# Projections split into two 64-row halves that run beside each other, with the score maxima one PSUM bank at a time

## The chip, the cores and the metric

The kernel runs on one core of one Trainium2 chip. The metric is device time in microseconds (us) of one execution of the whole program. Four compute engines matter here: TensorE (PE in the profile, its weight loads are PEld), VectorE (DVE), ScalarE (ACT) and GpSimd (POOL). SyncE (SP) issues nearly all the DMAs, in program order. Each engine works through its own instructions in program order.

## The reference

Two layers, each of them an attention block and an MLP on a 2048 x 640 tensor, all in float32:

```
qkv = layernorm(x) @ wqkv                  # 640 -> 3 x 32 heads x 20
p   = softmax(q @ k.T * 20**-0.5)          # 32 heads, 2048 x 2048 each
x   = x + (p @ v) @ wo
h   = relu(layernorm(x) @ w1 + b1) ** 2    # 640 -> 1536
x   = x + h @ w2 + b2                      # 1536 -> 640
```

The weights of both layers are the same arrays. Every float32 operand of a projection is split into a high and a low part of a shorter format, and a product is the sum of three: high by high, high by low, low by high. So a projection over 640 = 5 x 128 rows is a chain of 15 matmuls into one PSUM bank.

## The kernel before, in words

A layer has three stages: `qkv` (projections), `attention`, and `add_heads` with `mlp`. The change lies in `qkv`.

**Projections.** `UNITS` lists 40 units of q and k (128 output columns by 512 tokens); the first 16 of them (`FIRST` = 4 column blocks for four token blocks) hold what heads 0 to 11 need. `proj_unit` (L302) runs the 15 matmuls of a unit at L307, 128 rows of the array, 512 columns. Its result goes to SBUF as a high and a low part (ACT copies at L273, POOL splits at L278 and L281) and by DMA to `d_qk`. Then 16 tiles of v follow, two chains of 15 matmuls each at L358, 320 columns wide (`v_unit`, L350). The projections use PSUM banks 6 and 7 in turn.

**Maxima.** The softmax needs the largest score of each query before the attention stage uses it. It is found from scores that are computed once more, with queries on the partitions: `by_queries` (L463, matmul at L466) multiplies 60 rows, either rows 0 to 59 or rows 64 to 123 of the array (`par` = 0 or 1), by 512 keys. The two values of `par` are two heads, and two such matmuls with different `par` run side by side in the upper and the lower half of the array. A maximum over 512 keys for 128 queries of one head is called a single here; a layer has 2048 of them. Those not done in `qkv` are done in `attention` by `smax` (L474, DVE at L478).

In `qkv` there are two ways. A plain one (`smax_two`, L482): two matmuls into two neighbouring banks, one reduction of both by DVE (L487). A double one covers 1024 keys: `step_two` (L491) multiplies by the difference of two key blocks (`kd`), ACT takes the positive part (L498); `both_two` (L501) multiplies by the first block, and DVE adds the two and reduces (L508). So a double gives four singles for four matmuls, two ACT and two DVE instructions. All of these use banks 0 to 5 in three pairs (`Twos`). I call the two matmuls with `par` = 0 and 1 that belong together a pair; a double has two pairs.

**Order.** The order on TensorE is the program's. While the projections are issued, `between` (L801) counts matmuls, and after every 8.2 (`PACE`; 11 while there are no doubles) `some` (L775) issues a round: a `both`, a plain, and a `step` for the next round, three pairs in all. After every fourth matmul the next step of `rest` is issued, which prepares the normalised and transposed input (`front`, L373: statistics and normalisation on DVE, 4 transposes at L388 per step). The lists `PLAIN` and `DOUBLE` (L659, L666) say which groups of 8 pairs or doubles come up after which unit; groups that haven't come up when the projections end are left to `attention`.

**Attention.** 32 blocks of 4 heads by 512 queries. For each of 16 key tiles: four score matmuls (L563, 62 rows, two side by side), four exponentials on ACT (L570), four matmuls with v in four column tiles (L575). The order is a written-out string (`ORDERS`, L859) in which maxima are strewn, at least 12 pairs in each eight key tiles as long as any are left.

Of the kernel before, what the change touches and what calls it, by code (L numbers as in the profile page):

```python
# [8 lines left out]
F32 = mybir.dt.float32  # L9
# [7 lines left out]
P = 128  # L17
# [3 lines left out]
H = 32  # L21
# [18 lines left out]
def tile_layers(  # L40
# [51 lines left out]

    ps_st = Ring(0, 1, 2, 3)
    ps_pj = Ring(6, 7)

    class Twos:


        def __init__(self):
            self.n = 0  # L100

        def two(self):
            self.n = (self.n + 2) % 6
            return banks[:, self.n : self.n + 2, :]

        def __call__(self, label):
            return self.two()[:, 0, :]

    ps_q = Twos()
# [192 lines left out]
    def proj_unit(pos, tb, between):  # L302
        dst = ps_pj("pj")
        n = 0
        for k in range(KD):
            for hw, hx in THREE:
                nc.tensor.matmul(  # L307
                    dst,
                    w_qk.piece(pos * 10 + hw * KD + k),
                    xt_[tb][k][:, hx, :],  # L310
                    start=(n == 0),
                    stop=(n == 3 * KD - 1),
                )
                n += 1
                between()
# [34 lines left out]
    def v_unit(tt, between):  # L350
        tb, i = divmod(tt, 4)
        v = slot([P, H, 32], F32, "v")
        nc.gpsimd.memset(v[:, :, DH:], 1.0)
        n = 0
        for hf in range(2):
            dst = ps_pj("pv_")
            for j, (k, (hx, hw)) in enumerate((k, t) for k in range(KD) for t in THREE):
                nc.tensor.matmul(  # L358
                    dst[:, :HALF],
                    xt_[tb][k][:, hx, i * P : (i + 1) * P],  # L360
                    w_v.piece(k * 4 + hw * 2 + hf),
                    start=(j == 0),
                    stop=(j == 3 * KD - 1),
                )
                n += 1
                between()
            nc.scalar.copy(
                v[:, hf * 16 : hf * 16 + 16, :DH],
                dst[:, :HALF].rearrange("p (h d) -> p h d", d=DH),
            )  # L370
        return lambda: dma(nc.sync, d_v[tt * P : (tt + 1) * P], v)

    def front(tb, x_src, bank):  # L373

        rows = [row_tile(x_src, tb * 4 + i) for i in range(4)]
        yield
        mvs = []
        for x in rows:
            mvs.append(stats(x))
            yield  # L380
        for x, mv in zip(rows, mvs):
            normalise(nc.vector, x, mv)
            yield
        res = []
        for k in range(KD):
            dst = bank("xt")
            for i in range(4):
                nc.tensor.transpose(  # L388
                    dst[:, i * P : (i + 1) * P], rows[i][:, k * P : (k + 1) * P], ident
                )  # L390
            t = slot([P, 2, QB], F32R, "xnT")
            (split_on_pool if tb > 1 else split_to)(t[:, 0, :], t[:, 1, :], dst)
            res.append(t)
            if k == KD - 1:
                xt_[tb] = res
            yield

    def fronts(steps):


        for n, f in enumerate(steps):
            for m, _ in enumerate(f):
                if m == 7 and n + 1 < len(steps):
                    next(steps[n + 1])
                yield
# [76 lines left out]
    def smax_two(t, p, sub, c):  # L482

        dst = ps_q.two()
        for par in range(2):
            by_queries(dst[:, par, :], t, p, sub, c, par)
        nc.vector.tensor_reduce(  # L487
            maxima(t)[:, 2 * p : 2 * p + 2, sub, c], dst, axis=AX.X, op=ALU.max
        )

    def step_two(t, p, sub, x):  # L491

        dst = ps_q.two()
        res = [xtile("rl")[:, :QB] for _ in range(2)]
        for par in range(2):
            by_queries(dst[:, par, :], t, p, sub, x, par)
        for par in range(2):
            nc.scalar.activation(res[par], dst[:, par, :], AF.Relu)  # L498
        return res

    def both_two(t, p, sub, x, r):  # L501

        dst = ps_q.two()
        c = 2 * "de".index(x)
        for par in range(2):
            by_queries(dst[:, par, :], t, p, sub, c, par)
        for par in range(2):
            nc.vector.tensor_tensor_reduce(  # L508
                out=r[par],
                in0=dst[:, par, :],  # L510
                in1=r[par],
                scale=1.0,
                scalar=LEAST,
                op0=ALU.add,
                op1=ALU.max,
                accum_out=maxima(t)[:, 2 * p + par, sub, c : c + 1],
            )
# [125 lines left out]
    def prep_job():  # L643
# [7 lines left out]
        if jobs:  # L651
# [11 lines left out]
        ([], [(1, qb, c) for qb in (1, 2, 3) for c in (2, 3)]  # L663
         + [(2, qb, c) for qb in range(3) for c in range(NQB)]),
# [6 lines left out]
         [(1, 3, "d"), (1, 0, "e")]),  # L671
# [6 lines left out]
    PACE = 8.2  # L678
# [3 lines left out]
    def qkv(first, x_src, rest):  # L682
# [5 lines left out]
        state = {"pace": 0, "n": 0}  # L688
# [31 lines left out]
        def later(f=None):  # L720
            if f:
                pending.append(f)
            while len(pending) > (1 if f else 0):
                pending.pop(0)()

# [11 lines left out]
        def end_group(x):  # L737
            g, qb, c = x
            t = g * NQB + qb
            rest = groups + double + [w[0] for w in work + twos] + [w[0][0] for w in begun]  # L740
# [10 lines left out]
            for y in [y for y in k_t if y[0] == g < 2 and y not in use]:  # L751
                del k_t[y]
# [13 lines left out]
        def one():  # L766
            w = following(groups, work)
            if w:
                (g, qb, c), p, sub = w
                smax_two(g * NQB + qb, p, sub, c)  # L770
                done.add((g * NQB + qb, p, sub, c))
                if (p, sub) == PAIRS[-1]:
                    end_group(w[0])

        def some():  # L775
# [8 lines left out]
            if begun:  # L784
                w, r = begun.pop()
                (g, qb, x), p, sub = w
                t = g * NQB + qb
                both_two(t, p, sub, x, r)
                c = 2 * "de".index(x)
                done.update([(t, p, sub, c), (t, p, sub, c + 1)])  # L790
                if (p, sub) == PAIRS[-1]:
                    end_group(w[0])
            one()
            w = following(double, twos)
            if w:
                (g, qb, x), p, sub = w
                begun.append((w, step_two(g * NQB + qb, p, sub, x)))
            else:
                one()
# [461 lines left out]
```

## Time and profile before

| | |
|---|---|
| median of 3 runs | 3725.42 us (3721.52 to 3725.97) |
| the profiled execution | 3724.8 us, of which 3723.0 us are the span of the profile |
| granted TensorE clock | 0.997 |
| first `qkv` stage | 0 to about 361 us |
| first attention, then `add_heads` and `mlp` | to about 1449 us, to about 1878 us |
| second `qkv` stage | 1879 to 2205 us |
| second attention, then `add_heads` and `mlp` | to about 3295 us, to 3723 us |
| busy in the span | PE 3683.9, DVE 2791.9, ACT 2558.5, POOL 824.1 us |

The duration of a matmul in the profile runs from its start to its modelled end, and matmuls overlap. So the time that a matmul takes of TensorE is read from the distance of the starts, not from the duration. In the timeline, equal instructions in a row stand in one line: start, time from the first start to the last end, engine, line, operation, output and inputs, shapes, count; in brackets the idle time before and what ended it.

### The profile page before, as it was taken

Reading aid. Unit: us, or ns where it says so; the run is one execution under the profiler, and the core shown is the slowest. Engines: PE = TensorE matmul, PEld = TensorE weight load, DVE = VectorE, ACT = ScalarE, POOL = GpSimd, SP = SyncE. Lnnn points to the kernel's source line nnn. Section 1 sums busy time; section 2 is a strip of 40 time slices with the busy share of each in tenths; the row PEclk is TensorE's granted clock in tenths of the full one; section 3 lists DMA queues with packets and bytes.
Section 4 is the critical chain, followed back from the end, with each engine's and each line's share of the span. In section 5 each row is a group of like instructions: output and inputs, shape, how many; then the busy total and the mean of one; then the engine's idle time right before and its main releaser. Section 6 shows DMA issues by size and latency. Waiting matters only on the chain.

```text
span 3723.0 us, 64229 instructions
## 1 busy us (share of the span) xinstructions
PE 3683.9 (99%) x23572; PEld 2111.6 (57%) x23572; DVE 2791.9 (75%) x4799; ACT 2558.5 (69%) x4891; POOL 824.1 (22%) x914
## 2 busy tenths in 40 slices
PE   7999999999999999999999999999999999999999
PEld 5677344433443346989876763444334433378998
DVE  7788999999999993344567889999999999823443
ACT  2455999999999995122224459999999999941221
POOL 6430234322112211111153201121212121201110
PEclk9999999999999999999999999999999999999999
DMA  7564454432212136511265533222222111373111
GB/s 228 186 211 142 136 153 139 132 107 74 59 52 52 43 94 204 200 43 43 81 221 172 171 124 81 75 72 56 72 78 57 45 48 49 107 246 139 43 48 38
DMA packets 256531, 402.28 MB, mean 108 GB/s; under 512 B 67580, under 2 KB 114428, under 8 KB 256216
## 3 DMA queue, kind: packets, MB, share of 16 engines
q1 hardware_dynamic: 255384, 395.80, 34.3%
q8 instruction: 187, 3.06, 0.3%
q10 hardware_dynamic: 832, 2.37, 0.2%
q14 instruction: 128, 1.05, 0.1%
HBM read 261.22 MB, written 136.81 MB: 107 GB/s over the span
## 4 chain that ended last, share of the span: by engine, by line
PE 94%; DVE 3%; ACT 1%; DMA 1%; POOL 0%; issue 0%; SPq 0%; ACTq 0%; DVEq 0%; POOLq 0%
PE banks L575 27%; PE banks L296 20%; PE banks L563 20%; PE banks L466 15%; PE banks L307 6%; PE banks L358 4%; DVE mx L487 1%; DVE h L267 1%; PE banks L1047 0%; DVE bst L254 0%; DVE r L1074 0%; ACT h L266 0%; PE banks L388 0%; ACT r L1073 0%; DMA k<-d_qk 0%
## 5 line engine op out<-in xcount | busy, mean ns | idle before, releaser
L570 ACT ACTIVATE e<-banks 128x512 f32<-128x512 f32 x4096 | 2114.3, 604 | 63.4 <-PE banks L563 3.9
L478 DVE TENSOR_REDUCE mx<-banks 128x1 f32<-128x512 f32 x2940 | 1846.5, 684 | 188.1 <-PE banks L466 115.5
L466 PE MATMUL banks<-k,q 60*128 60x512 f32 x3744 | 1157.4, 436 | 5.4 <-DMA q<-d_qk 3.0
L563 PE MATMUL banks<-q,k 62*128 62x512 f32 x4096 | 1151.5, 435 | 2.1 <-DVE mx L487 1.7
L575 PE MATMUL banks<-e,vg 128*32 128x512 f32 x8192 | 1092.9, 605 | 0.1
L563 PEld LDWEIGHTS banks<-q,k 62*128 62x128 f32 x4096 | 600.5, 185 | 699.2 <-ACT e L570 665.8
L466 PEld LDWEIGHTS banks<-k,q 60*128 60x128 f32 x3744 | 537.4, 185 | 333.5 <-DVE mx L478 206.3
L296 PE MATMUL banks<-w,h 128*128 128x320 f32 x2304 | 360.0, 313 | 8.0 <-DVE h L267 4.3
L575 PEld LDWEIGHTS banks<-e,vg 128*32 128x32 f32 x8192 | 161.6, 108 | 358.2 <-issue 331.6
L498 ACT ACTIVATE rl<-banks 128x512 f32<-128x512 f32 x352 | 191.3, 596 | 247.9 <-PE banks L466 247.8
L296 PEld LDWEIGHTS banks<-w,h 128*128 128x128 f32 x2304 | 342.3, 189 | 17.4 <-DVE h L267 8.6
L296 PE MATMUL banks<-xnT,w 128*128 128x512 f32 x1440 | 330.0, 389 | 0.0
L307 PE MATMUL banks<-xnT,wqk 128*128 128x512 f32 x1200 | 319.8, 409 | 0.8 <-ACT xnT L266 0.4
L1073 ACT ACTIVATE r<-banks,b_t 128x512 f32<-128x512 f32 x96 | 66.1, 689 | 364.3 <-PE banks L296 362.9
L508 DVE CUSTOM_DVE_ANT_0 rl<-banks,rl 128x512 f32<-128x512 f32 x352 | 229.2, 689 | 112.4 <-PE banks L466 103.0
L296 PEld LDWEIGHTS banks<-xnT,w 128*128 128x128 f32 x1440 | 269.5, 188 | 55.2
L487 DVE TENSOR_REDUCE mx<-banks 128x2 f32<-128x1024 f32 x226 | 271.7, 1220 | 15.1 <-PE banks L466 14.3
L307 PEld LDWEIGHTS banks<-xnT,wqk 128*128 128x128 f32 x1200 | 217.0, 191 | 86.2 <-issue 43.3
L619 POOL TENSOR_TENSOR few<-few,minus_t 128x16 f32<-128x16 f32 x62 | 179.8, 2901 | 289.2 <-DMA few<-d_s 289.2
L630 POOL TENSOR_TENSOR o<-o 128x512 f32<-128x512 f32 x62 | 79.6, 1283 | 620.7 <-DMA o<-d_r 350.8
L1093 DVE TENSOR_TENSOR x<-banks,x 128x320 f32<-128x320 f32 x128 | 62.9, 492 | 184.4 <-PE banks L296 184.2
L278 POOL CAST mr<-nt 128x32 fp32r<-128x32 f32 x64 | 13.4, 210 | 801.5 <-DVE nt L534 801.5
(77 smaller groups left out, 1994.4 us busy)
## 6 DMA issues: line engine op xcount, KB each, us to landing
q<-d_qk SPq DMA_DIRECT2D x744, 80.0 KB
d_qk<-ev SPq DMA_DIRECT2D x80, 512.0 KB
k<-d_qk SPq DMA_DIRECT2D x468, 80.0 KB
x<-d_x SPq DMA_DIRECT2D x88, 320.0 KB
d_o<-ot SPq DMA_DIRECT2D x248, 80.0 KB
ot<-d_o SPq DMA_DIRECT2D x38, 512.0 KB
d_v<-v SPq DMA_DIRECT2D x32, 512.0 KB
vg<-d_v SPq DMA_DIRECT2D x32, 512.0 KB
```

What stands on the lines that cost most here:

```text
L296: nc.tensor.matmul(dst, a, b, start=(n == 0), stop=(n == last))
L307: nc.tensor.matmul(dst, w_qk.piece(pos * 10 + hw * KD + k), xt_[tb][k][:, hx, :], start=(n == 0), stop=(n == 3 * KD - 1),)
L358: nc.tensor.matmul(dst[:, :HALF], xt_[tb][k][:, hx, i * P : (i + 1) * P], w_v.piece(k * 4 + hw * 2 + hf), start=(j == 0), stop=(j == 3 * K ...
L466: nc.tensor.matmul(dst, q_t[t][b : b + 60, p, sub * P : (sub + 1) * P], k_t[t // NQB, c][b : b + 60, p, :], start=True, stop=True,)
L478: nc.vector.tensor_reduce(maxima(t)[:, 2 * p + par, sub, c : c + 1], dst, axis=AX.X, op=ALU.max)
L487: nc.vector.tensor_reduce(maxima(t)[:, 2 * p : 2 * p + 2, sub, c], dst, axis=AX.X, op=ALU.max)
L498: nc.scalar.activation(res[par], dst[:, par, :], AF.Relu)
L508: nc.vector.tensor_tensor_reduce(out=r[par], in0=dst[:, par, :], in1=r[par], scale=1.0, scalar=LEAST, op0=ALU.add, op1=ALU.max, accum_out= ...
L563: nc.tensor.matmul(dst, k_t[t // NQB, kt // 4][b : b + 62, p, (kt % 4) * P : (kt % 4 + 1) * P], q_t[t][b : b + 62, p, :], start=True, stop ...
L570: nc.scalar.activation(es[p][:, par, :], dst, AF.Exp, scale=SCALE)
L575: nc.tensor.matmul(acc[32 * h : 32 * h + 32, :], v_t[t // NQB, kt // 8][:, kt % 8, 32 * h : 32 * h + 32], es[p][:, par, :], start=(kt == 0 ...
L619: nc.gpsimd.tensor_tensor(few, few, minus_t, op=ALU.pow)
```

## The change

Every projection matmul with 128 rows becomes two with 64 rows: one for the upper half of the rows (0 to 63), one for the lower half. `chains` lists all 40 units and the 32 chains of v. Two counters run over them. The upper counter is ahead: an iteration issues the next upper half-matmul of chain n, and then the next lower half-matmul of an earlier chain, which adds to the bank that the upper rows of that chain have left. The lower counter follows 15 + 9 half-matmuls behind (`LAG` = 9). Between the last upper and the first lower half-matmul of a chain stands a tiny ACT copy (`mark`): it waits for the one, and the other waits for it. A chain of 15 matmuls becomes 30; there are 72 chains and 72 marks in a layer.

The maxima are now issued one matmul at a time (`single`): the one with `par` = 0 takes the place of an upper half-matmul, the one with `par` = 1 that of a lower one. Projections get the four banks 4 to 7, maxima (and the transposes of `front`) banks 0 to 3, one each. The counted pace is gone; `insert` keeps clocks (`now`) for PE, DVE and ACT in microseconds, written as constants (0.235 or 0.155 for an iteration, 0.58 to 0.7 for the work on a bank), and issues a matmul for a maximum only when the bank that comes next is free by these clocks. Up to two doubles are begun at a time. A plain is now two reductions of one bank each.

Of the `PLAIN` list four groups remain (64 singles a layer); all else that is listed for heads 0 to 11 is now `DOUBLE`, 22 groups instead of 11 (704 singles instead of 352). Fronts that run inside `qkv` make their transposes for two banks in one step, three steps in place of five.

The diff, cut to its core:

```
-    ps_pj = Ring(6, 7)
-
-    class Twos:
-
-
-        def __init__(self):
-            self.n = 0
-
-        def two(self):
-            self.n = (self.n + 2) % 6
-            return banks[:, self.n : self.n + 2, :]
-
-        def __call__(self, label):
-            return self.two()[:, 0, :]
-
-    ps_q = Twos()
+    ps_pj = Ring(4, 5, 6, 7)
+    ps_q = Ring(0, 1, 2, 3)
...
-    def proj_unit(pos, tb, between):
-        dst = ps_pj("pj")
-        n = 0
-        for k in range(KD):
-            for hw, hx in THREE:
-                nc.tensor.matmul(
-                    dst,
-                    w_qk.piece(pos * 10 + hw * KD + k),
-                    xt_[tb][k][:, hx, :],
-                    start=(n == 0),
-                    stop=(n == 3 * KD - 1),
-                )
-                n += 1
-                between()
...
+    def after(later, earlier):
+        tc.add_manual_dep(
+            later.ins,
+            earlier.ins.name,
+            mybir.DependencyInfo(mybir.DependencyClass.Sync, mybir.DependencyReason.DATA),
+            reason="lower rows add to the bank that the upper rows have left",
+        )
+
+    def product(ch, n, r):
+
+        what, a, b = ch["of"]
+        rows = slice(64 * r, 64 * r + 64)
+        k, t = divmod(n, 3)
+        if what == "qk":
+            hw, hx = THREE[t]
+            w = w_qk.piece(b * 10 + hw * KD + k)[rows]
+            x = xt_[a][k][rows, hx, :]
+            pair, width = (w, x), QB
+        else:
+            tb, i = divmod(a, 4)
+            hx, hw = THREE[t]
+            x = xt_[tb][k][rows, hx, i * P : (i + 1) * P]
+            pair, width = (x, w_v.piece(k * 4 + hw * 2 + b)[rows]), HALF
+        first, last = r == 0 and n == 0, r == 1 and n == 3 * KD - 1
+        if first:
+            ch["dst"] = ps_pj("pj")
+        m = nc.tensor.matmul(ch["dst"][:, :width], *pair, start=first, stop=last)
+        if n == 3 * KD - 1 and r == 0:
+            mark = nc.scalar.copy(mark_t[:, 0:1], mark_t[:, 1:2])
+            after(mark, m)
+            ch["upper"] = mark
+        if n == 0 and r == 1:
+            after(m, ch.pop("upper"))
+
+    def end_qk(pos, tb, dst):
...
+    def end_v(tt, hf, dst):
+        if hf == 0:
+            vs[tt] = slot([P, H, 32], F32, "v")
+            nc.gpsimd.memset(vs[tt][:, :, DH:], 1.0)
+        nc.scalar.copy(
+            vs[tt][:, hf * 16 : hf * 16 + 16, :DH],
+            dst[:, :HALF].rearrange("p (h d) -> p h d", d=DH),
+        )
+        if hf:
+            v = vs.pop(tt)
+            return lambda: dma(nc.sync, d_v[tt * P : (tt + 1) * P], v)
...
+    def front(tb, x_src, bank, each=1):
...
+        for k0 in range(0, KD, each):
+            ks = range(k0, min(k0 + each, KD))
+            dsts = [bank("xt") for _ in ks]
+            for k, dst in zip(ks, dsts):
+                for i in range(4):
+                    nc.tensor.transpose(
+                        dst[:, i * P : (i + 1) * P], rows[i][:, k * P : (k + 1) * P], ident
+                    )
+            for dst in dsts:
+                t = slot([P, 2, QB], F32R, "xnT")
+                (split_on_pool if tb > 1 else split_to)(t[:, 0, :], t[:, 1, :], dst)
+                res.append(t)
+            if len(res) == KD:
                 xt_[tb] = res
-            yield
+                rows.clear()
+            yield 0, len(res) < KD
...
-    def smax_two(t, p, sub, c):
-
-        dst = ps_q.two()
-        for par in range(2):
-            by_queries(dst[:, par, :], t, p, sub, c, par)
-        nc.vector.tensor_reduce(
...
+    def step_one(t, p, sub, x, par):
+
+        dst = ps_q("sm")
+        res = xtile("rl")[:, :QB]
+        by_queries(dst, t, p, sub, x, par)
+        nc.scalar.activation(res, dst, AF.Relu)
+        return res
...
+    def both_one(t, p, sub, x, par, r):
+
+        dst = ps_q("sm")
+        c = 2 * "de".index(x)
+        by_queries(dst, t, p, sub, c, par)
+        nc.vector.tensor_tensor_reduce(
+            out=r,
+            in0=dst,
+            in1=r,
+            scale=1.0,
+            scalar=LEAST,
+            op0=ALU.add,
+            op1=ALU.max,
+            accum_out=maxima(t)[:, 2 * p + par, sub, c : c + 1],
...
-        ([], [(1, qb, c) for qb in (1, 2, 3) for c in (2, 3)]
-         + [(2, qb, c) for qb in range(3) for c in range(NQB)]),
+        ([], []),
...
-         [(1, 3, "d"), (1, 0, "e")]),
+         [(1, 3, "d"), (1, 0, "e"), (1, 1, "e"), (1, 2, "e"), (1, 3, "e")]
+         + [(2, qb, c) for qb in range(NQB) for c in "de"]),
...
-        def one():
...
+        def takes(engine, ns, spot):
+            now[engine] = max(now[engine], now["pe"] + 0.25) + ns
+            busy[spot] = now[engine] + 0.12
+
+        def choose():
+
+            kind = state["last"]
+            if kind == "one" or not (groups or work):
+                if begun and begun[0]["ready"][0] < now["pe"] and len(begun[0]["r"]) == 2:
+                    return begun.pop(0) | {"kind": "both"}
+                if len(begun) < 2:
+                    w = following(double, twos)
+                    if w:
+                        begun.append({"kind": "step", "w": w, "r": [], "ready": []})
+                        return begun[-1]
             w = following(groups, work)
-            if w:
-                (g, qb, c), p, sub = w
-                smax_two(g * NQB + qb, p, sub, c)
-                done.add((g * NQB + qb, p, sub, c))
+            return {"kind": "one", "w": w} if w else None
...
+        def insert(par):
 
 
             while later_rows:
                 mrows_load(later_rows.pop())
-            if not (begun or double or twos):
-                for _ in range(3):
-                    one()
+            op = state["op"]
+            if bool(op) != bool(par):
+                return False
+            if now["pe"] < max(busy[b] for b in ps_q.coming(1)):
+                return False
+            if state["turn"] and not par:
+                if now["pe"] < max(busy[b] for b in ps_q.coming(2)):
+                    return False
+                now["pe"] += 1.2
+                for spot in ps_q.coming(2):
+                    takes("act", 0.6, spot)
+                    takes("dve", 0.7, spot)
+                step_rest()
+                return False
+            if not op:
+                op = state["op"] = choose()
+                if not op:
+                    return False
+                state["last"] = op["kind"]
+            single(op, par)
+            if par:
+                state["op"] = None
+            return True
+
+        def step_rest():
+            cost, state["turn"] = next(rest, None) or (0, False)
+            if cost:
+                now["dve"] = max(now["dve"], now["pe"]) + cost
...
-        def between(cost):
-            state["pace"] += cost
-            pace = PACE if double or twos or begun else 11
-            if state["pace"] >= pace:
-                state["pace"] -= pace
-                some()
...
+        chains = [{"of": ("qk", tb, pos)} for tb, pos in UNITS]
+        chains += [{"of": ("v", tt, hf)} for tt in range(NKT) for hf in range(2)]
+        N, LAG = 3 * KD, 9
...
+        def work_on(r):
+            n, m = divmod(at_now[r], N)
+            at_now[r] += 1
+            if n < len(chains):
+                product(chains[n], m, r)
+                if r and m == N - 1:
+                    end(n)
+
+        for j in range(len(chains) + 2):
+            if j < len(UNITS):
+                while UNITS[j][0] not in xt_:
+                    step_rest()
+                run(early, j)
+            while at_now[0] < (j + 1) * N and at_now[1] < len(chains) * N:
+                if not insert(0):
+                    work_on(0)
+                if not insert(1) and at_now[0] - at_now[1] > N + LAG + (not at_now[1]):
+                    work_on(1)
+                now["pe"] += 0.235 if j < len(UNITS) else 0.155
+                state["n"] += 1
+                if state["n"] % 4 == 0 and not state["turn"]:
+                    step_rest()
```

`single` issues one matmul of a plain, a `step` or a `both`, and books its bank with `takes` (0.62 us of DVE, 0.58 of ACT or 0.7 of DVE). `end` copies a finished chain out (`end_qk` and `end_v`, the code that followed the matmuls before). The stores of finished units are issued once per chain, and the groups of a list come up one chain later in the loop than before.

More of the change, by code (lines that the diff above doesn't have):

```diff
@@ L348, in proj_unit @@
         return store
[L350 to L373, printed above, removed]
+    vs = {}
+    def end_v(tt, hf, dst):
[10 more added lines that the diff above has]
+    def front(tb, x_src, bank, each=1):
         rows = [row_tile(x_src, tb * 4 + i) for i in range(4)]
-        yield
+        yield 0, False
         mvs = []
@@ L687, in qkv @@
         done.clear()
-        state = {"pace": 0, "n": 0}
+        state = {"n": 0, "turn": False, "op": None, "last": "one"}
+        now = {"pe": 0.0, "dve": 0.0, "act": 0.0}
+        busy = [0.0] * 8
         early, late, later_rows = {}, {}, []
@@ L739, in end_group @@
             t = g * NQB + qb
-            rest = groups + double + [w[0] for w in work + twos] + [w[0][0] for w in begun]
+            rest = groups + double + [w[0] for w in work + twos] + [o["w"][0] for o in begun]
             if t == 0:
@@ L851, in qkv @@
         load_v(0, 1)
-        for y in [y for y in k_t if y[0] == 1]:
+        for y in [y for y in k_t if y[0] == 1 or y[1] not in range(4)]:
             del k_t[y]
@@ L1175, in second @@
             yield
-        yield from front(3, d_x[1], ps_q)
+        yield from front(3, d_x[1], ps_q, 2)
     def begin_first():
@@ L1205, in begin_first @@
         rows.clear()
-        steps = [front(tb, x_in, ps_q) for tb in (1, 2, 3)]
+        steps = [front(tb, x_in, ps_q, 2) for tb in (1, 2, 3)]
         next(steps[0])
```

157 lines of the change are left out of this document (65 added, 92 removed).

## The prediction

> **What bounds the kernel now.** I read the page first, then the sums by stage, then timelines.
>
> ```profile
> span 3723.0 us, 64229 instructions
> PE 3683.9 (99%) x23572; PEld 2111.6 (57%) x23572; DVE 2791.9 (75%) x4799; ACT 2558.5 (69%) x4891; POOL 824.1 (22%) x914
> PE banks L575 27%; PE banks L296 20%; PE banks L563 20%; PE banks L466 15%; PE banks L307 6%; PE banks L358 4%; DVE mx L487 1%; DVE h L267 1%; PE banks L1047 0%; DVE bst L254 0%; DVE r L1074 0%; ACT h L266 0%; PE banks L388 0%; ACT r L1073 0%; DMA k<-d_qk 0%
> L478 DVE TENSOR_REDUCE mx<-banks 128x1 f32<-128x512 f32 x2940 | 1846.5, 684 | 188.1 <-PE banks L466 115.5
> L498 ACT ACTIVATE rl<-banks 128x512 f32<-128x512 f32 x352 | 191.3, 596 | 247.9 <-PE banks L466 247.8
> L487 DVE TENSOR_REDUCE mx<-banks 128x2 f32<-128x1024 f32 x226 | 271.7, 1220 | 15.1 <-PE banks L466 14.3
> ```
>
> The chain is TensorE nearly throughout, but that doesn't say that TensorE is what limits each stage. The sums by stage, for the second `qkv` and the second attention (columns: window, length, busy time by engine, clock, DMA share, GB/s):
>
> ```profile
> 1878.00:2207.00 329.00, 325.04 (x1695) 231.04 (x1694) 255.08 (x496) 135.14 (x258) 107.19 (x128) 1.00 0.55 177
> 2207.00:3295.00 1088.00, 1087.68 (x7604) 431.99 (x7603) 949.84 (x1563) 1056.12 (x2047) 201.90 (x186) 1.00 0.26 71
> ```
>
> In attention ACT is busy 1056 of 1088 us: ACT is the limit there. In `qkv` ACT has 135 and DVE 255 of 329 us: there TensorE is the limit. Counts: L487 226 / 2 = 113 plain pairs a layer, L498 352 / 2 / 2 = 88 doubles; 113 x 2 + 88 x 4 = 578 singles of 2048, and 1470 (L478 2940 / 2) are left to attention. Pairs in `qkv`: 113 + 2 x 88 = 289.
>
> **What a matmul costs.** Long unmixed runs stand in the MLP (start, length, engine):
>
> ```profile
> 1505.55 17.84 PE L296 MATMUL banks<-wo,ot 128*128 128x320 f32 x120
> 1523.23 20.59 PE L296 MATMUL banks<-xnT,w 128*128 128x512 f32 x90
> 1543.66 2.94 PE L296 MATMUL banks<-w,h 128*128 128x320 f32 x17
> ```
>
> From start to start: 17.68 / 120 = 0.1475 us for 320 columns, 20.43 / 90 = 0.227 for 512. Two half-height matmuls side by side, in attention:
>
> ```profile
> 1397.21 0.39 PE L563 MATMUL banks<-q,k 62*128 62x512 f32 x1
> 1397.45 0.39 PE L563 MATMUL banks<-q,k 62*128 62x512 f32 x1
> 1397.68 0.39 PE L563 MATMUL banks<-q,k 62*128 62x512 f32 x1
> ```
>
> One pair each 0.235 us. Now the rounds of `qkv`, first among q and k, then among v:
>
> ```profile
> 1983.90 2.12 PE L307 MATMUL banks<-xnT,wqk 128*128 128x512 f32 x8
> 1985.95 0.73 PE L466 MATMUL banks<-k,q 60*128 60x512 f32 x4
> 1986.52 0.40 PE L466 MATMUL banks<-kd,q 60*128 60x512 f32 x2
> 1986.85 2.12 PE L307 MATMUL banks<-xnT,wqk 128*128 128x512 f32 x8
> ...
> 2187.87 2.02 PE L358 MATMUL banks<-wv,xnT 128*128 128x320 f32 x12
> 2189.83 0.79 PE L466 MATMUL banks<-k,q 60*128 60x512 f32 x4
> 2190.46 0.39 PE L466 MATMUL banks<-kd,q 60*128 60x512 f32 x2
> 2190.78 2.17 PE L358 MATMUL banks<-wv,xnT 128*128 128x320 f32 x13
> ```
>
> Eight projections take 2.05 us (1983.90 to 1985.95), of which 8 x 0.227 = 1.82 are work; three pairs 0.90, of which 0.705 are work. Lost: 0.23 + 0.20 = 0.43 a round. Among v: 1.96 less 12 x 0.1475, and 0.95 less 0.705: 0.19 + 0.24 = 0.43 again. So going from full height to half height and back costs 0.43 us, with no wait for another engine in the rows. There are 88 rounds with a step and about a dozen with plain pairs alone; I count 100 changes of line in the timeline of the second `qkv`, and take 0.42: **42 us a layer**.
>
> The stage runs from its first projection to the first score of attention:
>
> ```profile
> 1879.07 9.64 PE L307 MATMUL banks<-xnT,wqk 128*128 128x512 f32 x40
> ...
> 2205.35 0.49 PE L563 MATMUL banks<-q,k 62*128 62x512 f32 x1 [0.20 <-DVE mx L487]
> 2206.48 0.73 PE L563 MATMUL banks<-q,k 62*128 62x512 f32 x4 [0.64 <-DVE mx L487]
> ```
>
> 326.3 us = 600 x 0.227 (136.2) + 480 x 0.1475 (70.8) + 289 x 0.235 (67.9) + 42 + 9.4 for one front's transposes and for waits on DMA and DVE.
>
> **The change part by part**, a layer.
>
> 1. *Changes of height go:* -42, all on the path, since TensorE limits the stage.
> 2. *Projections as halves side by side:* 0.235 for a pair instead of 0.227; for 320 columns I add the same 8 ns, 0.1555. The trace shows such pairs only overwriting their banks, never adding to them. Bounds: 0.227 (as one full matmul) and 2 x 0.227 (one half after the other). I take the pair's row. The lower counter ends 24 iterations after the upper one, so 624 iterations of 512 columns and 481 of 320: 146.6 + 74.8 instead of 136.2 + 70.8: +14.
> 3. *More maxima.* All that is listed would be 384 pairs, 95 more. How many come up in time? A double books 2 x 0.7 on the DVE clock, so 1.4 us, six iterations of 0.235, two of which are its own pairs. After unit 17, when the last 18 groups come up, 22 units with 15 x 0.235 = 3.5 us each are left; x doubles fit in a unit by 1.4x = 3.5 + 0.47x, x = 3.8, in all 83. Among v an inserted pair moves the clock by only 0.155, and ACT (0.6 for the copy of a chain, 1.16 for a double) sets the end: 0.6 + 1.16x = 2.33 + 0.31x, x = 2.0, in 33.6 chains 68. That is 151, as many as are left (144 and some 7 from before) with no gap at all. I take about 20 doubles as left over: 344 pairs, 55 more, +13 us. Bounds: 0 more (0 us) and 95 (+22).
> 4. *Fronts.* A step of transposes among full-height matmuls:
>
> ```profile
> 1893.01 1.17 PE L307 MATMUL banks<-xnT,wqk 128*128 128x512 f32 x4
> 1894.02 0.60 PE L388 MATMUL banks<-ident,x 128*128 128x128 f32 x4
> 1894.37 1.17 PE L307 MATMUL banks<-xnT,wqk 128*128 128x512 f32 x4
> ```
>
> Four transposes take 0.35, and 0.10 more is lost beside them (1.01 less 4 x 0.227): five steps, 2.25 us. Transposes stay at full height, so each step now pays the change of height: 2 x (0.70 + 0.43) + 0.35 + 0.43 = 3.0. +0.7 for one front in the second layer, +2.1 for three in the first.
>
> 5. *New waits.* The consumers, in the second `qkv`:
>
> ```profile
> 1986.58 0.69 DVE L508 CUSTOM_DVE_ANT_0 rl<-banks,rl 128x512 f32<-128x512 f32 x1 [0.39 <-PE banks L466]
> 1986.95 1.09 ACT L498 ACTIVATE rl<-banks 128x512 f32<-128x512 f32 x2 [1.80 <-PE banks L466]
> ...
> 1987.19 0.69 DVE L508 CUSTOM_DVE_ANT_0 rl<-banks,rl 128x512 f32<-128x512 f32 x1
> ...
> 1987.80 1.22 DVE L487 TENSOR_REDUCE mx<-banks 128x2 f32<-128x1024 f32 x1
> ```
>
> DVE takes 0.61 us for a `both`, ACT about 0.55 for a `step`: less than the 0.7 and 0.58 booked. But ACT starts 0.43 us after the pair at 1986.52, while the clocks count 0.25. In order of size: a double is booked at 1.4 us and needs 1.22, so a bank is mostly free earlier than booked. Each mark stands in ACT's queue behind up to two `step` copies and the copy of a finished chain; behind the lower half that waits for it stands all of TensorE. It has 9 iterations plus some 4 inserted ones, 3 us among q and k, and 9 x 0.1555 + 2.6 x 0.235 = 2.0 us among v, against 0.4 for the matmul, 1.1 for two copies, 0.2 (an estimate) for itself: close among v. SP's queue keeps its order; its loads come as late as before, counted in units. I take +6, from 0 to the price of the first rival below.
> 6. *The end of the stage:* no 1024-wide reductions stand before attention's first scores, -0.8.
> 7. *Attention.* With maxima and, at its end, without (ACT L570, then DVE L478):
>
> ```profile
> 1108.00:1176.00 68.00, 66.17 (x129) 1.00 0.24 62
> 1414.00:1448.00 34.00, 33.95 (x68) 1.00 0.53 172
> ...
> 1108.00:1176.00 68.00, 60.30 (x98) 1.00 0.24 62
> ```
>
> 129 exponentials cost 68 us beside 98 maxima, and 64.5 alone (0.5 each). So a maximum costs attention only 3.5 / 98 = 0.036 us. It keeps its least pace of 12 pairs, so they just end sooner. 110 fewer (55 pairs): -4. Moving maxima into `qkv` is thus no gain (0.1175 us each there); only the heights are.
>
> Sum, second layer: -42 + 14 + 13 + 0.7 + 6 - 0.8 - 4 = -13. First layer, with 1.4 more for its fronts: -11.7. Together -24.8: 3724.8 (profiled execution, 0.6 below the median of 3725.42) becomes **3700**.
>
> **The rivals.**
>
> *Waits in TensorE's order eat more than the heights gave* (slower). Before, a round found six banks and a wait was rare:
>
> ```profile
> PEld banks L466 <- DVE mx L487: 6.8, 21, 0.9
> ```
>
> Now an order laid down by constants meets four banks; the constants count 0.25 us from matmul to consumer where the rows show 0.43. If each of 344 pairs a layer waits a third of that 0.18, or each of 72 marks 0.29, it is +21 a layer above my sum: 3742. It turns the sign from 0.036 us a pair on. Against it: ACT and DVE are booked longer than they run. 16%.
>
> *A half-height iteration takes longer than the pairs of attention* (slower). A change of 0.011 us in 2 x 1105 iterations is all of the gain. Among v an iteration issues four instructions (two weight loads, two matmuls) in 0.1555 us, 39 ns each, for 100 us on end. The densest stretch in this trace is
>
> ```profile
> 1874.33 1.47 PE L388 MATMUL banks<-ident,x 128*128 128x128 f32 x12
> 1875.56 2.88 PE L296 MATMUL banks<-w,h 128*128 128x320 f32 x18
> ```
>
> 24 instructions in 1.23 us, 51 ns each. At that pace 481 iterations cost 0.205: +24 a layer, 3748. Or adding banks get in each other's way; one half after the other (0.454, and 0.295 for 320 columns) would be +204 a layer, 4110. Against it: full matmuls that add (0.227) take no longer than pairs that overwrite (0.235). 12%.
>
> [...]
>
> *The waits take about the gain:* within 0.2% of no change, which is 7.4 us and about what a measurement of this kernel can tell: +9 to +16 a layer more than my 6. 14%.
>
> *Better:* the clocks also spare the 9 us a layer of old waits and new ones stay near zero: -30 in all on top, some 3675. 10%.
>
> **How the numbers follow.** Forecast (3682 to 3717) 48%. Faster by over 0.2%: 48 + 10 = 58%. Within: 14%. Slower: 16 + 12 = 28%. The range of 8 in 10 reaches from 3678 (part of the better case) up to 3752, over the bound of the first rival and the issue price of the second; outside are one half after the other and the sequencer's price.
>
> **What would show it.** The half-height projections: 4320 matmuls; starts 0.235 and 0.155 apart in pairs. Second `qkv`: about 317 us from first projection to first score, with some 344 pairs. Singles in attention: 2940 - 220 = 2720. Long waits of PE on `mark`, or on `rl` or `mx` of DVE, would show the first rival; wider starts without a wait the second. I am wrong if the heights' 0.43 us isn't a cost of changing, so that rows of 64 pay it elsewhere.

## The result, and the profile after

The changed kernel takes 3764.61 us (median of 4 runs, 3757.93 to 3767.03) against 3725.18 before: a ratio of 1.0105, 95% interval 1.0087 to 1.0122. It is slower, by 39 us, where I forecast 25 us less; it lies some 13 us above my range. The profiled execution took 3757.93 us.

The page after, the lines that answer to those of before:

```profile
span 3756.1 us, 68961 instructions
PE 3654.3 (97%) x25738; PEld 2184.0 (58%) x25738; DVE 2707.9 (72%) x5036; ACT 2663.6 (71%) x5222; POOL 824.5 (22%) x914
PE banks L570 27%; PE banks L558 20%; PE banks L285 20%; PE banks L474 15%; PE banks L320 10%; DMA k<-d_qk 1%; SPq L76 1%; DMA q<-d_qk 1%; DVE h L256 0%; PE banks L1110 0%; DVE r L1137 0%; ACT h L255 0%; POOL xnT L270 0%; ACT r L1136 0%; PE banks L394 0%
L486 DVE TENSOR_REDUCE mx<-banks 128x1 f32<-128x512 f32 x3028 | 1903.9, 684 | 286.8 <-PE banks L474 206.7
L474 PE MATMUL banks<-k,q 60*128 60x512 f32 x3563 | 1247.3, 431 | 55.5 <-DMA k<-d_qk 34.0
L503 DVE CUSTOM_DVE_ANT_0 rl<-banks,rl 128x512 f32<-128x512 f32 x535 | 349.3, 689 | 121.7 <-PE banks L474 107.2
```

Three things stand out. TensorE is busy 30 us less in a span 33 us longer. In the chain stand DMA of `k`, DMA of `q` and the SP queue, 3% together, where before only `k` stood, with 0%. And the matmuls of the maxima (now L474) have 55 us of idle time before them, most of it ended by a DMA; before it was 5 us. The waits of TensorE over the whole span, longest first (waited in total, times, longest), say which:

```profile
PE banks L474 <- DMA k<-d_qk: 34.0, 2, 17.9
PE banks L474 <- DMA q<-d_qk: 32.6, 10, 9.4
PE banks L1257 <- POOL x L251: 10.1, 1, 10.1
PE banks L320 <- DMA wv<-d_wv: 6.3, 2, 5.5
PE banks L320 <- DVE xnT L256: 3.3, 1, 3.3
PE banks L285 <- DVE h L256: 3.1, 15, 0.8
PE banks L394 <- DVE x L251: 3.0, 7, 1.1
PE banks L474 <- DVE mx L486: 2.5, 2, 2.2
```

Before, the same list has 10.2 for the first normalisation (the line with POOL), next to nothing for `k` and `wv`, and for `q`:

```profile
PE banks L466 <- DMA q<-d_qk: 3.0, 4, 1.1
```

So 70 us of waits for loads are new. Waits on a bank (`mx`) are 2.5 us, and waits on a mark don't occur.

By stage (qkv from the first projection to attention's first score, attention from there to the start of its last matmul with v), in us of the profiled execution of each kernel, those of the experiments included:

| kernel | qkv 1 | attention 1 | qkv 2 | attention 2 | span |
|---|---|---|---|---|---|
| before | 345.7 | 1088.7 | 326.3 | 1090.5 | 3723.0 |
| after | 332.1 | 1108.9 | 340.5 | 1106.0 | 3756.1 |
| a1_hold_qkv | 325.9 | 1141.1 | 300.1 | 1139.8 | 3777.4 |
| a2_hold_att | 333.5 | 1116.0 | 339.7 | 1110.5 | 3771.8 |
| a3_hold_all | 323.1 | 1134.6 | 297.1 | 1135.5 | 3763.3 |
| a4_keys_early | 337.5 | 1089.2 | 343.7 | 1088.3 | 3732.8 |
| b1_loads_early | 321.6 | 1095.0 | 303.6 | 1096.6 | 3687.1 |
| b2_whole_height | 482.3 | 1096.7 | 466.1 | 1101.5 | 4016.3 |
| b3_before_pace13 | 345.4 | 1139.3 | 325.7 | 1139.2 | 3818.7 |
| b4_before_keys_late | 345.2 | 1113.0 | 327.5 | 1115.3 | 3770.2 |
| c1_hold_10 | 336.0 | 1087.4 | 306.7 | 1092.7 | 3693.1 |
| c2_lag_2 | 324.8 | 1100.4 | 299.3 | 1102.9 | 3698.9 |

The first qkv gains 13.6, the second loses 14.2, the attentions lose 20.2 and 15.5; the rest makes -3.2.

What such a wait looks like, in the timeline of TensorE in the second qkv and then at the start of the first attention:

```profile
1900.65 8.48 PE L320 MATMUL banks<-xnT,wqk 64*128 64x512 f32 x72
1914.45 0.76 PE L474 MATMUL banks<-k,q 60*128 60x512 f32 x1 [5.32 <-DMA q<-d_qk]
...
360.66 0.50 PE L558 MATMUL banks<-q,k 62*128 62x512 f32 x2
379.01 0.99 PE L474 MATMUL banks<-k,q 60*128 60x512 f32 x2 [17.85 <-DMA k<-d_qk]
```

One matmul of a maximum waits for its tile, and all of TensorE stands behind it. SP's queue at the first of these stalls:

```profile
1902.64 3.71 SPq L76 DMA_DIRECT2D d_qk<-ev  x2
1906.45 2.64 SPq L76 DMA_DIRECT2D k<-d_qk  x6
1909.22 3.14 SPq L76 DMA_DIRECT2D q<-d_qk  x6
```

Two stores go out over 3.7 us, since the second waits for its data (DVE's last write of it ends at 1905.95); then six loads of `k`, six of `q`. The last `q` is issued at 1912, the maximum wanted it at 1909.1. Six loads took SP 2.64 us of issue here and six more 3.14, so each about half a microsecond, in order. And the stall costs more than its length. The windows of the stall, of what follows, and of the time after that (window, length, busy time by engine, clock, DMA share, GB/s):

```profile
1909.10:1914.40 5.30, 0.03 (x2) 0.00 (x0) 0.32 (x2) 0.67 (x2) 0.00 (x0) 0.97 0.70 189
1914.40:1921.00 6.60, 6.07 (x27) 4.84 (x29) 4.50 (x7) 0.00 (x0) 0.00 (x0) 0.51 0.16 61
1921.00:1926.00 5.00, 5.00 (x46) 4.45 (x44) 4.09 (x8) 0.93 (x3) 0.00 (x0) 1.00 0.45 134
```

After 5.3 us without work the granted clock is 0.51 for 6.6 us, by my estimate some 3.3 us of work lost (half of 6.6).

### The profile page after: what moved, and what is told of

Same layout as the page of the kernel before. It is cut to its first block, busy times and chain, and to the rows that moved or that the text cites. A ratio compares the mean times of both kernels' runs of the same rounds, so it can differ in the third digit from the quotient of the medians.

```text
span 3756.1 us, 68961 instructions
## 1 busy us (share of the span) xinstructions
PE 3654.3 (97%) x25738; PEld 2184.0 (58%) x25738; DVE 2707.9 (72%) x5036; ACT 2663.6 (71%) x5222; POOL 824.5 (22%) x914
## 4 chain that ended last, share of the span: by engine, by line
PE 92%; DMA 2%; DVE 2%; POOL 1%; SPq 1%; ACT 1%; issue 0%; ACTq 0%; POOLq 0%; DVEq 0%
PE banks L570 27%; PE banks L558 20%; PE banks L285 20%; PE banks L474 15%; PE banks L320 10%; DMA k<-d_qk 1%; SPq L76 1%; DMA q<-d_qk 1%; DVE h L256 0%; PE banks L1110 0%; DVE r L1137 0%; ACT h L255 0%; POOL xnT L270 0%; ACT r L1136 0%; PE banks L394 0%
## 5 line engine op out<-in xcount | busy, mean ns | idle before, releaser
L486 DVE TENSOR_REDUCE mx<-banks 128x1 f32<-128x512 f32 x3028 | 1903.9, 684 | 286.8 <-PE banks L474 206.7
L474 PE MATMUL banks<-k,q 60*128 60x512 f32 x3563 | 1247.3, 431 | 55.5 <-DMA k<-d_qk 34.0
L474 PEld LDWEIGHTS banks<-k,q 60*128 60x128 f32 x3563 | 584.6, 186 | 334.8 <-DVE mx L486 209.2
L503 DVE CUSTOM_DVE_ANT_0 rl<-banks,rl 128x512 f32<-128x512 f32 x535 | 349.3, 689 | 121.7 <-PE banks L474 107.2
L320 PE MATMUL banks<-xnT,wqk 64*128 64x512 f32 x2400 | 408.8, 409 | 3.3 <-DVE xnT L256 3.3
L570 PEld LDWEIGHTS banks<-e,vg 128*32 128x32 f32 x8192 | 161.6, 108 | 357.9 <-issue 332.1
L495 ACT ACTIVATE rl<-banks 128x512 f32<-128x512 f32 x539 | 289.8, 600 | 109.0 <-PE banks L474 99.1
L320 PEld LDWEIGHTS banks<-xnT,wqk 64*128 64x128 f32 x2400 | 309.5, 195 | 41.2 <-DVE xnT L256 3.7
L320 PE MATMUL banks<-wv,xnT 64*128 64x320 f32 x1920 | 206.1, 311 | 6.3 <-DMA wv<-d_wv 6.3
L320 PEld LDWEIGHTS banks<-wv,xnT 64*128 64x128 f32 x1920 | 195.5, 189 | 8.8 <-DMA wv<-d_wv 7.5
```

The lines of the kernel that those rows point to most:

```text
L320: m = nc.tensor.matmul(ch["dst"][:, :width], *pair, start=first, stop=last)
L474: nc.tensor.matmul(dst, q_t[t][b : b + 60, p, sub * P : (sub + 1) * P], k_t[t // NQB, c][b : b + 60, p, :], start=True, stop=True,)
L486: nc.vector.tensor_reduce(maxima(t)[:, 2 * p + par, sub, c : c + 1], dst, axis=AX.X, op=ALU.max)
L495: nc.scalar.activation(res, dst, AF.Relu)
L503: nc.vector.tensor_tensor_reduce(out=r, in0=dst, in1=r, scale=1.0, scalar=LEAST, op0=ALU.add, op1=ALU.max, accum_out=maxima(t)[:, 2 * p + ...
L570: nc.tensor.matmul(acc[32 * h : 32 * h + 32, :], v_t[t // NQB, kt // 8][:, kt % 8, 32 * h : 32 * h + 32], es[p][:, par, :], start=(kt == 0 ...
```

## The experiments

The theory: halves beside each other are the gain that I worked out, but the loads of the maxima now come too late, in qkv and at the start of attention. The rivals: half-height iterations or bank waits cost the time; or the loads are only where it shows.

**a1_hold_qkv**: in qkv, a group comes up only 14 us (by the order's own clock) after its tiles were loaded.

```diff
-                x = todo.pop(0)
+                x = todo[0]
                 tiles(x)
+                g, qb, c = x
+                cs = [c] if c in range(4) else [c, 2 * "de".index(c)]
+                got = max([k_at[g, i] for i in cs] + [q_at[g * NQB + qb]])
+                if now["pe"] < got + HOLD:
+                    return None
+                todo.pop(0)
...
```

> In qkv a group of maxima comes up only 14 us (by the order's clock) after the loads of its key and query tiles were issued; all else as changed. Theory of late loads: the waits of TensorE on loads of q in the two qkv stages (13.7 and 17.1 us in stalls of 3 us and more) go, and with each of the six stalls the 6 us at half clock behind it, some 3 us of work each: 31 + 19 us off, 3705 to 3715. Rival, that half-height iterations or bank waits are what costs time: the loads were only where the same time showed, 3750 to 3765.

Measured 3777.07 us, ratio 1.0143 (1.0128 to 1.0158): slower. But the stages part the two effects: the second qkv falls from 340.5 to 300.1, below the 326.3 of before, and waits for `q` fall from 32.6 us to

```profile
PE banks L478 <- DMA q<-d_qk: 7.5, 5, 2.8
```

Attention grows by 32 and 34 us. The theory holds for qkv; in attention something that I hadn't priced appears, and the whole time lies outside both of my ranges.

**a2_hold_att**: in attention, a maximum is issued only 14 key tiles after the loads of its tiles.

```diff
                 if (t // NQB, c) not in k_t or t not in q_t:
                     return
+                if tile_now[0] < max(k_in[t // NQB, c], q_in[t]) + 14:
+                    return
```

> In attention a maximum is issued only 14 key tiles after the load of its key or query tile was issued; all else as changed. Theory of late loads: the two stalls on key tiles at the start of each attention stage (17.9 and 16.1 us) go, and half clock behind them, 3718 to 3726. Rival, that attention's start has to wait for key tiles in any case (scores need them too): the stall moves to the scores, 3750 to 3765.

Measured 3775.35 us, 1.0138 (1.0123 to 1.0153). The waits for `k` are gone, and attention is still longer, 1116.0 and 1110.5. My expectation failed, and so did the rival: no score waits for a load.

**a3_hold_all**: both, and

```diff
-                at(early, n, lambda k=k: w_v.load(k))
+                at(early, n - 3, lambda k=k: w_v.load(k))
...
```

> Both of these, and the weights of v loaded three units earlier in the second layer (a stall of 5.5 us). Theory of late loads: the effects add up, 50 + 36 + 8 us off, 3665 to 3685, below the kernel before, since the changes of height that fell away are then a clear gain. Rival, that half-height iterations cost more: not below 3715.

Measured 3764.85 us, 1.0112 (1.0097 to 1.0127). The second qkv is better still, 297.1, and the longest wait for a load in the whole run is 1.4 us; attention takes 1135. So the time falls into the rival's range (not below 3715), but qkv speaks against the rival's cause. The windows of its attention show why that is longer, ACT's exponentials and then DVE's maxima, the first three of the first attention:

```profile
341.00:409.00 68.00, 66.35 (x132) 1.00 0.45 122
409.00:477.00 68.00, 62.93 (x123) 1.00 0.53 148
477.00:545.00 68.00, 62.78 (x123) 1.00 0.53 157
...
341.00:409.00 68.00, 13.68 (x22) 1.00 0.45 122
409.00:477.00 68.00, 60.72 (x98) 1.00 0.53 148
477.00:545.00 68.00, 60.43 (x98) 1.00 0.53 157
```

For most of the first 68 us there are no maxima, which had to wait. From then on it is 123 exponentials beside 98 maxima; before it was 129 beside 98. The order makes up for the late start with mostly 13 pairs in eight key tiles instead of 12. But DVE makes 98 in 68 us at either pace, so the exponentials pay.

**b3_before_pace13** tests that alone, in the kernel before:

```diff
-            n = min(max(round(state["debt"]), 12), 16)
+            n = min(max(round(state["debt"]), 13), 16)
```

> The kernel before with one number changed: in attention at least 13 pairs of maxima in eight key tiles instead of 12. Theory that DVE limits attention from there on: 123 exponentials in 68 us instead of 129 as long as maxima last (98 in 68 us in either case), then 0.5 us each: 1020 + 100 us, some 1120 instead of 1089 a layer, 3780 to 3790. If a maximum cost only the 0.036 us of the prediction, the pace wouldn't matter: 3725.

Measured 3821.81 us, 1.027 (1.0253 to 1.0287). Its exponentials and its maxima, in a window of the first attention:

```profile
632.00:700.00 68.00, 62.58 (x122) 1.00 0.58 173
...
632.00:700.00 68.00, 61.41 (x99) 1.00 0.58 173
```

Attention takes 1139 instead of 1089, with the same number of maxima. My 1120 had counted 1846 exponentials beside the 1470 maxima; in the trace it is 1815, in 1018 us, and the other 233 take 121. At either pace DVE makes no more than 98 or 99 maxima in 68 us, so I take it as the limit: 68 / 98 = 0.69 us a maximum. Whether DVE itself sets this rate or the banks that its matmuls wait for, no run parts.

**a4_keys_early**: key tiles 1 and 3 of heads 8 to 11, which doubles don't load (they use 0, 2 and the differences), are loaded in qkv.

```diff
+            if a == 6:
+                for c in (1, 3):
+                    load_k(2, c, True)
             if a == 10:
                 load_v(0, 0)
```

> As changed, but the key tiles 1 and 3 of heads 8 to 11, which only maxima that are left over need singly, are loaded while the seventh tile of v is made. Theory of late loads, in the form that these two tiles are what attention's first maxima wait for: the 17.9 and 16.1 us go without any holding back, 3718 to 3728. If other tiles or the queue are the cause: 3750 to 3765.

Measured 3723.38 us (median of 10; the profiled one, 3734.6, is the longest of them), ratio 0.9995 (0.9985 to 1.0005). Three lines give back all that the change had lost, 41 us; they bring no gain over the kernel before, and the waits for `q` in qkv stay (35.2 us). Attention has no wait for a load and takes 1089.2 and 1088.3. So it was these two tiles: maxima that qkv left over need them, and attention begins to load them only in its first key tiles.

**b4_before_keys_late** is the converse: the kernel before gives up its key tiles of heads 8 to 11 at the end of qkv.

```diff
-        for y in [y for y in k_t if y[0] == 1]:
+        for y in [y for y in k_t if y[0] in (1, 2)]:
```

> The kernel before, but the key tiles of heads 8 to 11 that qkv has loaded are given up at its end, so that attention's first maxima wait for loads. Theory of late loads: a stall of TensorE of 10 to 18 us at the start of each attention stage, with half clock behind it, though nothing is split into halves: 3745 to 3770. Rival, that only the halves make a late load cost anything: 3725.

Measured 3771.25 us, 1.0131 (1.0116 to 1.0147). Nothing is split, and TensorE waits for loads at the start of attention, as in the changed kernel. In the first attention it waits for `k`:

```profile
PE banks L466 <- DMA k<-d_qk: 19.5, 3, 12.6
```

In the second the longest waits are 12.5 us for `q` and 7.3 for `k`. Attention takes 1113.0 and 1115.3, 24 and 25 us more than before.

**b1_loads_early** joins a1's hold, a4's loads and a3's earlier weights of v.

> The changed kernel with all three kinds of late loads mended without holding attention back: groups come up in qkv 14 us after their loads, key tiles 1 and 3 of heads 8 to 11 are loaded during the seventh tile of v, weights of v three units earlier. Theory (the halves are a gain of some 25 us a stage, and the loads that they outran took it back): qkv 323 and 298 us instead of 345.7 and 326.3 before, attention as before at 1089, so 3675 to 3685. Rival, that fewer maxima in qkv push attention over its least pace again, as in the two runs that held maxima back: attention 1100 to 1140 each, 3700 to 3765.

Measured 3689.17 us (4 runs, 3685.45 to 3691.84), ratio 0.9911 (0.9896 to 0.9926): faster than both kernels, by 33 us than before, and 4 us above the range that I expected. The first qkv takes 321.6, the second 303.6, attention 1095.0 and 1096.6. Attention stays 6 us above the 1089 expected: 1480 singles are left to it (before: 1470), and in its trace ten stretches of four key tiles hold 13 instead of 12. Where attention starts without a late load, 1464 singles left go with 1087.4 us (c1, first layer), 1470 with 1088.7 (before) and 1488 with 1102.9 (c2, second layer): some 0.65 us for each more.

**b2_whole_height** is b1 with full-height projections:

```diff
-        rows = slice(64 * r, 64 * r + 64)
+        rows = slice(0, P)
+        if r:
+            return
...
```

> As b1_loads_early, but every projection is one matmul of full height again, in the place of its upper half; the order of everything else is the same. So each pair of maxima among the projections now changes the height twice. Theory of the heights (0.43 us a round, no cost of halves as such): some 250 to 300 changes there and back a stage, 110 to 130 us more in each qkv than b1_loads_early, 3890 to 3940. Rival, that the gain in qkv came from the order (one bank at a time, clocks) and not from the heights: within 20 us of b1_loads_early.

Measured 4020.04 us, 1.0801 (1.0785 to 1.0817). The qkv stages grow by 161 and 162 us, the attentions by 2 and 5. Its timeline:

```profile
202.76 0.50 PE L475 MATMUL banks<-k,q 60*128 60x512 f32 x1
203.19 0.50 PE L321 MATMUL banks<-xnT,wqk 128*128 128x512 f32 x1
203.62 0.49 PE L475 MATMUL banks<-k,q 60*128 60x512 f32 x1
204.04 0.96 PE L321 MATMUL banks<-xnT,wqk 128*128 128x512 f32 x3
```

Each matmul between two changes takes 0.43 us from start to start, 0.2 over its work, as in the rounds of before. It came out above my 110 to 130, because the two matmuls of a pair often stand apart, each with changes of its own: each stage has 753 changes of height, 376 there and back, and 376 x 0.43 = 162 us. In b1 the second stage has 6.

**c1_hold_10** shortens b1's hold to 10 us, and takes a double where a plain is held back.

```diff
-            if kind == "one" or not (groups or work):
+            w = following(groups, work) if kind != "one" else None
+            if w:
+                return {"kind": "one", "w": w}
+            if True:
...
```

> b1_loads_early with 10 us instead of 14 between loads and maxima, and a double is taken where a plain is held back. So more maxima are made in qkv. Theory that attention is limited by DVE at 0.69 us a maximum above the least pace and by ACT below it: attention goes back from 1095 to 1089, qkv grows by some 3 us for the maxima and keeps short stalls of 1 to 2 us: 3680 to 3688. If 10 us are too short in the first layer, stalls on q of several us come back: 3695 to 3705.

Measured 3690.19 us, 0.991 (0.9895 to 0.9924), no different from b1 and between my two ranges. Attention does fall, to 1087.4 and 1092.7, but the first qkv grows by 14: waits for `q` go from 8.0 to 18.0 us in all. 10 us are too short there.

**c2_lag_2** is b1 with a smaller lag.

```diff
-        N, LAG = 3 * KD, 9
+        N, LAG = 3 * KD, 2
```

> b1_loads_early with the lower halves 2 instead of 9 half-matmuls behind the upper ones, so that each lower chain starts right after the mark's matmul. Theory that marks cost nothing at 9: TensorE now waits for each of 72 marks a layer, 0.4 us for the matmul's end and 0.2 for ACT, less 2 to 3 iterations, so 0.2 to 0.6 us each, 15 to 40 us a layer: 3720 to 3770. If the marks hold up TensorE at 9 already, or ACT's queue is what sets the wait, little changes from 9 to 2: 3690 to 3700.

Measured 3699.1 us, 0.9925 (0.9909 to 0.9942), in the range that I gave for little change. My price of a mark was wrong:

```profile
PE banks L320 <- ACT mark_t L322: 3.4, 10, 1.0
```

Ten waits in both layers, 3.4 us, with the slack almost gone. Half the time one half of the array works for a maximum anyway, or the other half still adds to an earlier bank; that this is what covers the mark is argued, not shown. The second qkv is even shorter (299.3), and attention longer, as 12 more singles are left to it.

## Why the prediction was wrong

*Heights, -42 a layer (part 1): right.* With about as many maxima as before (571 matmuls of them instead of 578) the second qkv is 23 us shorter in b1 and 29 in a3, where fewer loads are late; parts 1, 2, 4 and 6 add up to 28. b2 shows the price of a change in each row, and that without the halves the new order is no gain.

*Halves at 0.235 us (part 2): right, adding too, and if anything too high.* A long run of pairs that add, in the first qkv of the changed kernel, and a window out of another in the second:

```profile
34.74 6.89 PE L320 MATMUL banks<-xnT,wqk 64*128 64x512 f32 x58
41.56 0.33 PE L394 MATMUL banks<-ident,x 128*128 128x128 f32 x1
...
1902.61 6.52 PE L320 MATMUL banks<-xnT,wqk 64*128 64x512 f32 x56
```

29 pairs in 6.82 us, 0.235 each, with the change of height to the transpose behind them. In the window, without such a change, the last of 28 pairs starts 6.13 us after the first (6.52 less the last matmul's 0.39): 0.227 each, as long as one full matmul. Among v, seven iterations of 320 columns take 1.07 us (1.37 less the last matmul's 0.30), 0.153 each, 38 ns an instruction:

```profile
2195.17 1.37 PE L320 MATMUL banks<-wv,xnT 64*128 64x320 f32 x15
```

So the second rival, a slower iteration, falls, and one half after the other (0.454) with it: two adding halves took 0.235 us. The sequencer's price, which my range leaves outside, is shown by no run; an iteration among v took 0.153 us, 38 ns an instruction.

*More maxima (part 3): mis-sized.* 539 `step` instructions are 135 doubles a layer, not 156: 300 pairs, 11 more than before instead of 55. Not all fit in, as I thought, but far fewer did than I took. That spared qkv time, but it left 41 doubles a layer to attention, and I had not looked at which key tiles those need.

*New waits (part 5): the step that failed.* I wrote that SP's "loads come as late as before, counted in units". In the changed kernel the lower half of a unit ends 24 iterations after the upper one, units pass faster (a later unit of q and k takes 5.0 us, before 5.6), and six loads of `q` still stand behind stores that wait for their data and six loads of `k`: 32.6 us of waits for `q` and 6.3 for `wv`, 3.0 and 0 before. a1 and a3 show that these loads were late; how much of it is the lag and how much the faster units, no run parts. I had added 6 a layer and looked for them on marks and banks, where there are nearly none.

*Attention (part 7): failed too.* That "a maximum costs attention only 3.5 / 98 = 0.036 us" holds while the least pace suffices and the tiles of the maxima are there. Left-over doubles need two key tiles that before came with the plain groups: 34.0 us of waits. a4 shows that this alone makes the difference between slower and level: with the tiles there, 41 us come back. And where the order has to go above its least pace, because maxima start late or more of them are left, a maximum more costs some 0.65 us (c1, b1, c2), and a pace one pair higher throughout costs 50 us a layer (b3). The row that I read it from, 98 maxima in 68 us, already had the rate that b3 doesn't exceed; I took ACT alone as the limit.

*The first rival* had the shape right, a wait in TensorE's order, but named the wrong releaser. Of the 39 us lost, the new waits for loads are 70 us and half clock some more (the granted clock over the span is 0.987, before 0.997); against them stand the heights. b1, with the loads mended, is at 3689, 11 below my forecast: the core of the change is the gain that I worked out, if its loads are moved with it. That the number comes so near is in part luck: in b1 the 13 us a layer for more maxima in qkv are not paid, and attention takes 6 us more than before instead of 4 less.

## What to carry to other kernels

When work is moved on an engine that works in order, list for each moved matmul the loads that it needs, where they stand in their queue and which stores stand ahead: a tile that used to come as a by-product of other work is lost when that work is replaced. A stage's price for one more item depends on which engine is at its limit there: read it at the pace that the kernel will have, not at the one that it has. And when a change with a sound core measures slower, look at the waits by releaser first; here three lines made up the whole loss.

## What the runs showed of the hardware

In the second qkv of the changed kernel TensorE's granted clock was 0.50 or 0.51 after each of five stalls of 3.15 to 5.48 us: for 6.0 to 6.4 us after four of them (the first is shown above), and for 10.2 after the shortest. By these figures a stall of 5 us costs about 8 (5 and half of 6), an estimate. The time after the shortest stall, and a stretch at half clock in the first qkv, shortly after a stall of 2.16 us that ended at 55.99:

```profile
1965.35:1975.50 10.15, 9.70 (x40) 7.31 (x42) 3.54 (x6) 1.97 (x4) 1.88 (x2) 0.50 0.84 260
57.20:60.60 3.40, 3.40 (x18) 2.74 (x18) 3.33 (x9) 0.19 (x1) 1.43 (x4) 0.50 0.12 49
```

So half clock also followed stalls of 2.16 and 3.15 us, for 3.4 and 10.2 us. What sets whether the clock is halved, and for how long, no run parts.

Half-height matmuls that add to their bank also went at full pace beside ones that overwrite another, in the second qkv of the changed kernel:

```profile
1922.78 0.39 PE L474 MATMUL banks<-k,q 60*128 60x512 f32 x1
1922.80 1.07 PE L320 MATMUL banks<-xnT,wqk 64*128 64x512 f32 x6
1923.49 0.39 PE L474 MATMUL banks<-k,q 60*128 60x512 f32 x1
```

From one maximum to the next, with projections in the other places, three iterations in 0.71 us, 0.237 each, against 0.227 in the unmixed run above.
